# Causal attention tiles of 64 queries in a two-layer attention and FFN kernel: shared score products, a slot ring, and a new order

## The chip, the cores and the metric

The kernel runs on one core of one Trainium2 chip. The metric is device time in microseconds, the median of several executions of the same program. The engines are named as the profile names them: PE (TensorE matmul) and PEld (its weight loads), DVE (VectorE), ACT (ScalarE), POOL (GpSimd) and SP (SyncE, which here issues nearly all DMAs).

## What is computed

Two kinds of layer alternate, attention and a gated FFN, each applied twice to a sequence of 2048 rows of 512 columns (bf16). Attention has 32 heads of 16 columns and works in four segments of 512 rows; each segment has causal softmax attention inside itself and, beside it, a linear memory of the segments before. Cut to what matters:

```python
for s in range(4):                                   # segments of L = 512 rows
    qs, ks, vs = q[:, :, s], k[:, :, s], v[:, :, s]  # 32 heads, Dh = 16
    logits = einsum('bhqd,bhkd->bhqk', qs, ks) * Dh ** -0.5 + causal_mask
    a_dot = einsum('bhqk,bhkd->bhqd', softmax(logits), vs)
    pq = phi(qs)                                     # t + 1 where t > 0, else exp(t)
    a_mem = einsum('bhld,bhde->bhle', pq, M) / (einsum('bhld,bhd->bhl', pq, z)[..., None] + 1e-6)
    outs.append(g * a_mem + (1 - g) * a_dot)         # g = sigmoid(beta), one per head
    pk = phi(ks)
    M = M + einsum('bhld,bhle->bhde', pk, vs); z = z + einsum('bhld->bhd', pk)
...
x = x + A(layernorm(x));  x = x + (gelu(n @ w_gate) * (n @ w_up)) @ w_down   # n = layernorm(x)
x = x + A(layernorm(x));  x = x + (gelu(n @ w_gate) * (n @ w_up)) @ w_down   # n = layernorm(x)
```

## The kernel before

The work is cut into eight steps k: segments 0 to 3 of the first attention and FFN, then of the second. The class `Att` holds the attention of one step and `Ffn` its FFN. All weights, all of x and the memory stay on chip.

**Order.** Nothing is ordered by a scheduler on the chip: `order` walks through the program once, on the host, with a clock for every engine (`Clocks`, `Engine`) and assumed costs. PE's queue is filled one call or product at a time, and the order in which instructions are written is the order in which each engine runs them. Work for PE waits in a list of `Item`s, each with a due time and a condition; a call to `score` goes first where the backlog of exps on ACT is short. Work for the other engines is posted with the time from which it is ready and a slack; if it is posted on two engines, the one that serves it first takes it. The numbers in `POLICY` are due times and slacks. If no item can be opened while scores are still left, the loop writes a product on the tile `warm`, which computes nothing that is used (a fill).

**Attention.** Heads go in quartets. The 128 rows of a q or k block b hold eight heads of 16 rows; four of them, one in each strip of 32 partitions, run side by side in PE as tiles of 32 rows ("rows"). The even heads (par 0) use the upper 16 rows of each strip from `kf`; the odd ones (par 1) use all 32 rows of `kB`, a copy of the keys whose even heads' rows are zero. The copy is made by DVE for steps under 5 (`kb_dve`) and by SP's DMAs, four for each block, after that.

A score product has 128 keys as stationary operand and queries as columns. The causal triangle is cut at 128 queries: for one head, 512 + 384 + 256 + 128 = 1280 columns, five rounds of 256 (`PIECES`), each for a quartet. Eight steps, four blocks, two heads per strip and five rounds make 320 rounds, always two in one `score` call. A call writes four PSUM banks; two exps of 1024 columns (ACT, L1246) move them into slots of `pt_all`, of which there are ten, and POOL zeroes what lies over the diagonal (`affine_select`, L1252). A flush (`flush_item`, L838) multiplies the probabilities of a quartet with its values `vaug`, whose 17th column makes the softmax sum; it runs as four tiles of 32 columns of the array ("columns"), 1280 columns in six groups of four matmuls, and gives its slots back. There are 64 flushes.

**Tilings.** `Clocks.tiling` tracks three tilings of PE: rows, columns and whole. `product` (L396, L399) writes a 128x128 product either whole (L399) or as four column tiles (L396): in columns if PE is in columns already, or if it is in rows and a flush is pending. The memory's products (denominators `den_mm` L671, numerators `num` L694, updates `m` L748) and the transposes `turn_item` (L485 to L487) are always whole.

**Norms.** `Norm` makes statistics and the normalised rows `xn` on DVE; SP's transposing DMAs (`turn_later`) turn them into `xnT`, or PE does for the keys in `BY_PE` (FFN norms of steps 0, 1 and 7).

**phi.** ACT makes the exponential e, POOL cuts it at 1 (L643), DVE adds (L629). The buffers for xn, e and am are separate.

Of the kernel before, what the change touches and what calls it, by code (L numbers as in the profile page):

```python
# [20 lines left out]
H = 32  # L21
# [9 lines left out]
VW = H * (DH + 1)  # L31
SCALE = DH ** -0.5
# [9 lines left out]
NO_DIAG = 1  # L42
# [6 lines left out]
XN_BUFS = 4  # L49
FILL = 2  # L50
# [4 lines left out]
    flush_wait=31.24, piece_slack=21.809, kb_slack=10.712, mem_slack=-1.256, margin=2.578, qk_due=1.366,  # L55
    e_q=-0.208, e_k=1.104, exp_slack=-8.673, e_slack=10.49, phi_slack=11.84, gelu_slack=-0.257, act_evict=7.504,
    first_evict=-5.126, gate_step=0.0, up_due=1.343, up_step=0.018, down_due=3.044, down_step=0.196,
    upd_due=-0.283, v0_due=-0.631, x1_at=2.428, x2_at=1.735, x3_at=6.651, x3_load=17.614, cut_slack=-5.505,
    direct=4, gelu_tiles=1, phi_pool=0, kb_dve=5, rounds=2, early=8.837, starve=0.645, ahead=0.994, near=-6.896,
    cap=1, soon=6.003)  # L60
# [68 lines left out]
class Clocks:  # L129
# [3 lines left out]
    SMALL = 0.025  # L133
    SWITCH = 0.097
# [89 lines left out]
class Item:  # L224


    def __init__(self, due, ready, ops, done, kind, ps, after="start"):
        self.after = after
        self.due, self.ready, self.ops, self.done, self.kind, self.ps = due, ready, ops, done, kind, ps
        self.posted = 0.0  # L230
# [12 lines left out]
class Policy:  # L243
    def __init__(self, values):
        self.__dict__.update(values)


def order(pol, nc, cst, seg, wrk, psp, A_x, A_wq, A_wk, A_wv, A_wo, A_beta, B_x, B_w_gate, B_w_up, B_w_down, out):
# [29 lines left out]
    for cols in (slice(0, P), slice(P, D)):  # L278
        load(w_att["k"][:, :, cols], w_view(A_wk)[:, :, cols])
        load(w_att["q"][:, :, cols], w_view(A_wq)[:, :, cols])  # L280
# [44 lines left out]
    kBs = [cst.tile([P, KT, L], BF16, name=f"kB{i}") for i in range(SETS)]  # L325
    for kB in kBs[1:]:
        nc.vector.memset(kB[:], 0.0)
    maskB = cst.tile([P, 1], F32, name="maskB")
    nc.vector.reduce_sum(out=maskB[:], in_=bd[:, 16:P:32], axis=mybir.AxisListType.X)

    tmp_e = cst.tile([P, H], F32, name="tmp_e")
    tmp_e2 = cst.tile([P, H], F32, name="tmp_e2")
    cden = cst.tile([P, H], BF16, name="cden")
    macc = cst.tile([P, 4, P], F32, name="macc")
    zacc = cst.tile([P, 4], F32, name="zacc")
    vaugs = [cst.tile([P, TPS, VW + 15], BF16, name=f"vaug{i}")[:] for i in range(SETS)]
    vaugs.append(gel_sb[:].rearrange("p f l -> p (f l)")[:, 0:TPS * (VW + 15)].rearrange("p (t v) -> p t v", t=TPS))

    def by_head(va):
        return va[:, :, 0:VW].rearrange("p t (h e) -> p t h e", e=DH + 1)  # L340


    def gate_constants():
        nc.vector.tensor_scalar(out=cden[:], in0=tmp_e[:], scalar1=1.0, scalar2=None, op0=ALU.add)
        nc.vector.tensor_scalar(out=tmp_e2[:], in0=tmp_e2[:], scalar1=1.0, scalar2=None, op0=ALU.add)


    def later_constants():
        def column(va):
            nc.vector.tensor_copy(out=by_head(va)[:, :, :, DH], in_=cden[:].unsqueeze(1).to_broadcast([P, TPS, H]))  # L350
            nc.vector.memset(va[:, :, VW:], 0.0)

        for n, va in enumerate(vaugs[-1:] + vaugs[:-1]):
            ck.dve.post(12.0 + 3.0 * n, NORMAL, (0.4, lambda va=va: column(va), None))

# [34 lines left out]
    def product(out, lhsT, rhs, start=True, stop=True):  # L390

        if ck.mode == "columns" or ck.mode == "rows" and any(it.kind == 'flush' for it in items):
# [4 lines left out]
        else:  # L397
            ck.tiling("whole")
            nc.tensor.matmul(out, lhsT=lhsT, rhs=rhs, start=start, stop=stop)  # L399

# [8 lines left out]

    xn_slots = Slots(ck, XN_BUFS)  # L410

    class Norm:
# [35 lines left out]
        def start(self, ready):  # L448
            self.xnT = seg.tile([P, KT, L], BF16, tag=self.tag, bufs=1, name="xnT")
            for j in range(TPS):  # L450
                xn_slots.take(lambda i, j=j: self.row(j, i, max(ready, ck.pe)))

        def normed(self, j, i):
            xn = seg.tile([P, D], BF16, tag=f"xn{i}", bufs=1, name="xn")
            nc.vector.tensor_scalar(out=xn[:], in0=x_sb[:, self.tt0 + j, :], scalar1=self.mv[:, j, 0:1],  # L455
# [3 lines left out]
        def row(self, j, i, ready):  # L459
            xn = Box(lambda: self.normed(j, i))  # L460

            def landed(t):
                xn_slots.back(i, t)
                self.left -= 1
                if not self.left:
                    ev[self.key] = t

            def told(t):
                if self.key in BY_PE:
# [5 lines left out]
            ck.dve.post(ready, self.slack, (Slowed(0.405, 0.17), xn, told))  # L475

        def turn_item(self, j, xn, t, landed):
# [4 lines left out]
            def turned():  # L482
                return ps()[:, 0:half].bitcast(BF16).rearrange("p (k t) -> p k t", t=P)

            ops = [(Clocks.MM[512] / 2, whole(lambda: nc.tensor.matmul(  # L485
                ps()[:, half:L], lhsT=warm[:], rhs=wide[:, 0:2, :], start=True, stop=True)))] * FILL
            ops += [(Clocks.MM[128], whole(lambda kt=kt: nc.tensor.transpose(  # L487
                turned()[:, kt, :], xn()[:, kt * P:(kt + 1) * P], ident[:]))) for kt in range(KT)]
            return Item(-0.5, lambda: t + Engine.LATENCY <= ck.pe + FILL * Clocks.MM[512] / 2, ops,
# [20 lines left out]
    class Att:  # L510
        def __init__(self, k):
            self.k, self.s, self.tt0 = k, k % NSEG, TPS * (k % NSEG)
            self.norm = Norm(("xnTa", k), self.tt0, f"xnTa{k % 2}", NORMAL, lambda: k < 2 or ("qkv", k - 2) in ev)
            self.vaug = vaugs[(k - 1) % SETS if k else SETS]
            self.ab, self.aT, self.amT, self.n_qkv, self.n_am, self.n_num = {}, None, {}, 0, 0, 0
# [7 lines left out]
        def add_items(self):  # L523
# [5 lines left out]
            def first():  # L529
                if k:  # L530
                    self.q, self.kf = (seg.tile([P, KT, L], BF16, tag=f"{n}{k % SETS}", bufs=1, name=n)
                                       for n in ("q", "kf"))
                    self.kB = kBs[k % SETS]
                else:
                    self.q, self.kf, self.kB = (wd_sb[:, KT * i:KT * (i + 1), :] for i in range(3))
# [839 lines left out]
```

## Time and profile before

| | |
|---|---|
| median of 3 runs | 554.04 us (553.85 to 556.86) |
| the profiled execution | 554.69 us, span 553.0 us, granted PE clock 1.00 |
| exps on ACT (L1246) | 320, 1025 ns each |
| masks on POOL (L1252) | 192 of 128x512, 681 ns; 128 of 128x256, 446 ns |
| score matmuls (L822) | 1536 |
| flush matmuls (L838) | 1536 |
| POOL's cuts of e (L643) | 48, 1545 ns each |

The profiled execution's own time is 1.7 us over its span, which is what the profiler covers. In the lines of the profile, a group names line, engine, operation, tiles written and read, shape and count, and behind the bars busy time, mean duration and idle time before it. Matmuls overlap, so the time that one costs PE is read from the start of one to the start of the next and not from its duration.

### The profile page before, as it was taken

The numbers are of one execution on the slowest core, as the hardware profiler recorded it, in microseconds if no ns is written. First come the engines' busy times: TensorE is split into PE (matmuls) and PEld (weight loads), VectorE is DVE, ScalarE is ACT, GpSimd is POOL, SyncE is SP. The second block draws the span as 40 slices with busy tenths as digits, with TensorE's granted clock in tenths as the row PEclk, the third lists the DMA queues.
The fourth block names the chain that finished last, engine by engine and source line by source line (L and its number), as shares of the span: only waits on it lengthen the run. The fifth ranks groups of instructions, "written<-read, shape, count | busy, mean of one in ns | idle before, by whom it ended". The sixth has DMA issues, their size and how long they took to land.

```text
span 553.0 us, 21391 instructions
## 1 busy us (share of the span) xinstructions
PE 544.8 (99%) x9257; PEld 269.2 (49%) x9257; DVE 449.3 (81%) x837; ACT 445.1 (81%) x570; POOL 280.4 (51%) x410
## 2 busy tenths in 40 slices
PE   8999999999999999999999999999999999999997
PEld 4444454454544545444444445444554446445544
DVE  7999899889978999689896898968978697776062
ACT  5899899999999998999999899999539987930500
POOL 2687767278617877237882356836427264300000
PEclk9999999999999999999999999999999999999999
DMA  8355701510131022301142021021321004100001
GB/s 260 47 118 129 180 3 40 163 13 3 30 59 22 13 50 50 60 3 40 24 56 42 2 47 35 12 41 22 50 67 31 4 4 97 21 2 21 19 2 39
DMA packets 66463, 26.56 MB, mean 48 GB/s; under 512 B 55104, under 2 KB 66368, under 8 KB 66368
## 3 DMA queue, kind: packets, MB, share of 16 engines
q1 hardware_dynamic: 65936, 24.92, 21.3%
q8 instruction: 72, 1.18, 0.9%
q10 hardware_dynamic: 432, 0.27, 0.2%
q14 instruction: 23, 0.19, 0.1%
HBM read 9.71 MB, written 2.10 MB: 21 GB/s over the span
## 4 chain that ended last, share of the span: by engine, by line
PE 79%; DVE 17%; issue 2%; DMA 1%; ACT 0%; POOL 0%; DVEq 0%
PE ps L396 42%; PE ps L399 21%; PE ps L822 7%; PE ps L838 5%; DVE st L425 3%; DVE xn L455 2%; DVE x_sb L908 2%; DVE byq L853 2%; PE ps L694 1%; DVE ab L861 1%; PE ps L748 1%; DMA phik<-e 1%; DVE q L386 1%; DVE mv L433 1%; DVE kf L386 1%
## 5 line engine op out<-in xcount | busy, mean ns | idle before, releaser
L1246 ACT ACTIVATE pt<-ps 128x1024 bf16<-128x1024 f32 x320 | 309.3, 1025 | 44.4 <-PE ps L822 34.5
L1252 POOL TENSOR_SCALAR_AFFINE_SELECT pt<-pt 128x512 bf16<-128x512 bf16 (+1 forms) x320 | 185.7, 587 | 182.8 <-ACT pt L1246 180.2
L968 DVE TENSOR_TENSOR gel_sb<-gel_sb,ps 128x512 bf16<-128x512 bf16 x112 | 76.4, 686 | 47.2 <-PE ps L396 27.5
L643 POOL TENSOR_SCALAR e<-e 128x512 bf16<-128x512 bf16 x48 | 74.1, 1545 | 4.3 <-ACT e L625 1.8
L396 PE MATMUL ps<-xnT,wu_sb 128*32 128x512 bf16 x1280 | 73.5, 380 | 0.0
L396 PE MATMUL ps<-xnT,wg_sb 128*32 128x512 bf16 x1144 | 68.9, 380 | 0.3 <-DVE x_sb L908 0.3
L908 DVE TENSOR_TENSOR x_sb<-x_sb,ps 128x512 bf16<-128x512 bf16 (+1 forms) x68 | 43.0, 643 | 23.9 <-PE ps L399 16.0
L396 PE MATMUL ps<-wd_sb,gel_sb 128*32 128x512 bf16 (+1 forms) x1060 | 60.5, 369 | 0.0
L853 DVE STREAM_TRANSPOSE byq<-ps 128x512 f32<-128x512 f32 x64 | 45.0, 706 | 6.9 <-PE ps L838 6.7
L396 PEld LDWEIGHTS <-wu_sb 128*32 128x32 bf16 x1280 | 32.8, 97 | 33.4 <-issue 2.8
L399 PE MATMUL ps<-wd_sb,gel_sb 128*128 128x512 bf16 (+1 forms) x239 | 45.1, 342 | 0.0
L396 PEld LDWEIGHTS <-wg_sb 128*32 128x32 bf16 x1144 | 28.7, 97 | 28.6 <-issue 5.5
L838 PE MATMUL ps<-pt,vaug 128*32 128x256 bf16 (+1 forms) x1344 | 40.7, 256 | 0.4 <-ACT gel_sb L946 0.3
L425 DVE BATCH_NORM_STATS2 st<-x_sb 128x6 f32<-128x512 bf16 x60 | 40.5, 674 | 0.2
L1020 ACT ACTIVATE gel_sb<-gel_sb 128x512 bf16<-128x512 bf16 x70 | 38.4, 628 | 0.1
L399 PE MATMUL ps<-xnT,wg_sb 128*128 128x512 bf16 x162 | 37.8, 380 | 0.0
L396 PEld LDWEIGHTS <-gel_sb 128*32 128x32 bf16 x1060 | 26.0, 97 | 24.2 <-issue 4.6
L838 PEld LDWEIGHTS <-vaug 128*32 128x32 bf16 x1344 | 31.1, 97 | 10.8 <-issue 2.9
L386 DVE CAST gel_sb<-ps 128x512 bf16<-128x512 f32 x46 | 30.8, 683 | 5.3 <-PE ps L396 4.9
L399 PEld LDWEIGHTS <-gel_sb 128*128 128x128 bf16 x239 | 22.6, 97 | 17.2
L455 DVE TENSOR_SCALAR xn<-x_sb,mv,rs 128x512 bf16<-128x512 bf16 x64 | 30.0, 522 | 1.2 <-POOL rs L443 0.9
L822 PE MATMUL ps<-q,kf 16*128 16x256 bf16 (+1 forms) x672 | 30.7, 255 | 0.0
(129 smaller groups left out, 738.2 us busy)
## 6 DMA issues: line engine op xcount, KB each, us to landing
wg_sb<-in_B_w_gate_dram SPq DMA_DIRECT2D x8, 224.0 KB, 4.4
wu_sb<-in_B_w_up_dram SPq DMA_DIRECT2D x8, 224.0 KB, 4.4
wd_sb<-in_B_w_down_dram SPq DMA_DIRECT2D x7, 256.0 KB, 3.0
x_sb<-in_A_x_dram SPq DMA_DIRECT2D x3, 512.0 KB, 8.1
out_dram<-x_sb SPq DMA_DIRECT2D x12, 128.0 KB, 1.9
xnT<-xn SPq DMA_TRANSPOSE x48, 2.5
kB<-kf SPq DMA_DIRECT2D x48, 16.0 KB, 1.8
wv_sb<-in_A_wv_dram SPq DMA_DIRECT2D x1, 512.0 KB, 7.2
```

What stands on the lines that cost most here:

```text
L386: ck.dve.post(ck.made(), slack, (0.673, lambda: nc.vector.tensor_copy(out=dst(), in_=src()), end), taken=taken)
L396: nc.tensor.matmul(out[r], lhsT=lhsT[:, r], rhs=rhs, start=start, stop=stop, tile_position=(0, 32 * c))
L399: nc.tensor.matmul(out, lhsT=lhsT, rhs=rhs, start=start, stop=stop)
L425: nc.vector.bn_stats(out=self.st6[:, 0, :], in_=x_sb[:, self.tt0 + j, :])
L643: return lambda: eng.tensor_scalar(out=e[0][:], in0=e[0][:], scalar1=1.0, scalar2=None, op0=ALU.min)
L822: nc.tensor.matmul(ps_all[:, pair[unit // 2], o:o + n], lhsT=lhsT[rows, b, P * ki:P * ki + P], rhs=self.q[rows, b, q0:q0 + n], start=True, ...
L838: nc.tensor.matmul(ps()[32 * j:32 * j + 32, q0:q0 + n], lhsT=self.vaug[:, ki, h * (DH + 1):h * (DH + 1) + 32], rhs=pt_all[:, slot, unit, c ...
L853: nc.vector.transpose(out=self.byq[:, par, :, :].rearrange("p a c -> p (a c)"), in_=ps()[:])
L908: ck.dve.post(ck.made(), slack, (0.15 + 0.00104 * (c1 - c0), lambda: nc.vector.tensor_tensor(out=xt, in0=xt, in1=ps()[:, 0:c1 - c0], op=AL ...
L968: ck.dve.post(ck.made(), NORMAL, (0.683, lambda: nc.vector.tensor_tensor(out=g, in0=g, in1=ps()[:], op=ALU.mult), lambda t: (ps.read(t), e ...
L1246: nc.scalar.activation(out=pt_all[:, s0, :, :].rearrange("p (h u) c -> p h (u c)", h=2), in_=ps_all[:, p0[0]:p0[1] + 1, :], func=ACT.Exp, ...
L1252: nc.gpsimd.affine_select(out=half, in_=half, pattern=[[0, w], [1, P]], compare_op=ALU.is_ge, fill=0.0, base=0, channel_multiplier=-1)
```

## The change

- **Tiles of 64 queries.** The part of each head's triangle that lies over full 64-query blocks is laid out in four rounds (`FULL`). What is left is, for each 128 keys, the square over which the diagonal begins: the first 64 keys against the first 64 queries of the same 128. For these, the keys of the even head and of the odd head are put side by side as one stationary operand of 128 columns, so that one product serves both heads (`PAIRED`, the round `SHARED`). A pair of heads has 9 rounds where it had 10: 288 in all.
- **Keys.** In place of `kB` there is `kx`, per block and 128 keys three times 64 columns: the first 64 keys of the even head, then all keys of the odd head. Two copies with a mask as scale make it, on DVE, POOL or ACT (`on_any`).
- **Values.** The shared round's probabilities hold the even head in partitions 0 to 63 and the odd head in 64 to 127. `vz` holds the values for it, half of its rows for the one and half for the other kind of head, zero elsewhere; two SP DMAs per step fill it from `vaug`, after the last flush of the step before. `vaug` is ordered by even and odd heads. A flush has ten groups of four matmuls (six with `vaug`, four with `vz`), again 1280 columns, and waits for `vz`.
- **Slots.** Slot number = round number modulo 10, in a fixed order. One exp takes a pair of banks with both rounds of a call and writes half of each of two neighbouring slots.
- **Masks.** One per round where there is a diagonal (`DIAG`), on POOL; the shared round is masked by DVE (one multiplication with `tri`) or by POOL (two halves).
- **Choice of engine.** xn of attention norms, the cut of e and the addition of the memory's part to aT may be done by DVE or POOL (`on_dve_or_pool`). xn, e and am share six buffers.
- **PE's tilings and turns.** The memory's products go through `product`, and `columns=1` lets products after a score always be in columns. With `pe_turns=1` PE turns segment 1's attention rows, without fills.
- **Order.** A new `POLICY`; values products need only their own 128 rows of xnT, and wo and down products may be opened when their first operand is there (`soon`). The first weights of q and k come in halves of 256 columns.

```diff
-ROUNDS = 5
-STEPS = 8 * ROUNDS
-PIECES = [[(0, 0, 256, 0)], [(0, 256, 256, 0)], [(1, 128, 256, 0)], [(3, 384, 128, 0), (1, 384, 128, 128)],
-          [(2, 256, 256, 0)]]
+ROUNDS = 9
+STEPS = KT * ROUNDS
+C = P // 2
+FULL = [[(0, 64, 256, 0)], [(1, 192, 64, 0), (0, 320, 192, 64)], [(1, 256, 256, 0)], [(3, 448, 64, 0), (2, 320, 192, 64)]]
+DIAG = [1, 1, 0, 2]
+SHARED = len(FULL)
+PAIRED = [(ki, P * ki, C, C * ki) for ki in range(TPS)]
...
-        if ck.mode == "columns" or ck.mode == "rows" and any(it.kind == 'flush' for it in items):
+        if ck.mode == "columns" or ck.mode == "rows" and (pol.columns or any(it.kind == 'flush' for it in items)):
...
+    def on_dve_or_pool(ready, slack, later, fast, slow, emit, told):
+        taken = []
+        ck.dve.post(ready, slack, (fast, lambda: emit(nc.vector), told), taken=taken)
+        if later is not None:
+            ck.pool.post(ready, slack + later, (slow, lambda: emit(nc.gpsimd), told), taken=taken)
...
+    def by_pe(self):
+        return self.key in BY_PE or self.key[0] == "xnTa" and self.key[1] <= pol.pe_turns
...
+                    for which, c0, c1, src, costs in ((0, 0, C, lo[:, :, 0:C], (0.22, 0.9, 0.4)),
+                                                      (1, C, 3 * C, lo, (0.36, 1.6, 0.61))):
+                        on_any(ck.pe, pol.kb_slack if k else NORMAL, pol.kb_pool, pol.kb_act, costs, lambda t2: there(t2),
+                               self.kx[:, b, :, c0:c1], src, masks[:, which:which + 1])
...
+                    for a in range(2):
+                        ck.sp.post(ck.pe, pol.vz_slack, (0.62, lambda a=a: nc.sync.dma_start(
+                            out=half(vz, slice(C * a, C * a + C), a), in_=half(self.vaug, slice(0, C), a)), vz_sent))
+                def vz_sent(t):
+                    self.n_vz += 1
+                    t2 = max(t + 1.8, ck.dma + 1.2)
...
             def den_mm(j, b):
-                nc.tensor.matmul(dens()[:, j, b, :], lhsT=self.phiq[:, b, j * P:(j + 1) * P],
-                                 rhs=mem_state[k - 1][1][:, b, :], start=True, stop=True)
+                product(dens()[:, j, b, :], self.phiq[:, b, j * P:(j + 1) * P], mem_state[k - 1][1][:, b, :])
...
+                work = [(i + par * (SHARED + 1), self.vaug, *piece) for i, pieces in enumerate(FULL) for piece in pieces]
+                work += [(SHARED, vz, *piece) for piece in PAIRED]
+                for m, (i, va, ki, q0, n, c0) in enumerate(work):
+                    for j in range(4):
+                        g = (DH + 1) * (par * H // 2 + 4 * b + j)
+                        nc.tensor.matmul(ps()[32 * j:32 * j + 32, q0:q0 + n], lhsT=va[:, ki * VW + g:ki * VW + g + 32],
+                                         rhs=pt_all[:, places[i], j, c0:c0 + n], start=(m == 0),
+                                         stop=(m == len(work) - 1), tile_position=(0, 32 * j))
...
+    def mask_both(slot):
+        view = pt_all[:, slot, :, :].rearrange("p u (t c) -> p (u t) c", c=C)
+        nc.vector.tensor_tensor(out=view, in0=view, in1=tri[:].unsqueeze(1).to_broadcast([P, 4 * TPS, C]), op=ALU.mult)
...
+    def slot_of(k, t):
+        return (k * STEPS + t) % PT_SLOTS
```

More of the change, by code (lines that the diff above doesn't have):

```diff
@@ L1193, in open_item @@
     def open_item(got, bank):
-        it = min(got, key=lambda it: it.due)
+        it = min(got, key=lambda it: it.due())
         items.remove(it)
@@ L1266, in score, with exp, told @@
-        for a, t, places in flushes:
-            a.flush_item(t // (2 * ROUNDS), t // ROUNDS % 2, places, owner[a.k, t // ROUNDS])
+        s0, left = slots[0], [n]
+        for p, pair in enumerate(pairs):
+            score_banks.update(pair)
+            for i in pair:
+                banks[i] = 1e9
+            def exp(p=p, pair=pair):
+                nc.scalar.activation(
+                    out=pt_all[:, s0:s0 + 2, 2 * p:2 * p + 2, :].rearrange("p r h c -> p h r c"),
+                    in_=ps_all[:, pair[0]:pair[1] + 1, :].rearrange("p h (r c) -> p h r c", r=2), func=ACT.Exp, scale=SCALE)
+            def told(a, pair=pair):
+                score_banks.difference_update(pair)
+                for i in pair:
+                    banks[i] = a
+                left[0] -= 1
+                if not left[0]:
+                    for slot, t, done in marks:
+                        post_mask(slot, t, a, done)
+            ck.act.post(max(begun + 0.4, free), pol.exp_slack, (1.024, exp, told), table="exp")
```

424 lines of the change are left out of this document (229 added, 195 removed).

## The prediction

> **What bounds the kernel now.** I read the page first: busy line, slices and chain.
>
> ```profile
> PE 544.8 (99%) x9257; PEld 269.2 (49%) x9257; DVE 449.3 (81%) x837; ACT 445.1 (81%) x570; POOL 280.4 (51%) x410
> ...
> PE   8999999999999999999999999999999999999997
> ...
> ACT  5899899999999998999999899999539987930500
> ...
> PE 79%; DVE 17%; issue 2%; DMA 1%; ACT 0%; POOL 0%; DVEq 0%
> ```
>
> PE is busy in every slice, ACT drops out after slice 33, and the chain that ended last is PE for 79%. A busy PE is not yet a useful one, so next came the table by stretches:
>
> ```profile
> 0.00:20.00 20.00, 18.61 (x184) 8.47 (x188) 16.16 (x46) 14.40 (x24) 8.02 (x21) 1.00 0.59 185
> 20.00:60.00 40.00, 39.48 (x768) 18.79 (x760) 39.37 (x84) 36.91 (x44) 30.91 (x43) 1.00 0.63 118
> 200.00:250.00 50.00, 50.00 (x933) 24.02 (x929) 41.43 (x77) 45.88 (x61) 26.86 (x39) 1.00 0.24 40
> 350.00:400.00 50.00, 49.66 (x925) 24.26 (x924) 42.85 (x76) 42.42 (x57) 27.02 (x38) 1.00 0.22 33
> 500.00:525.00 25.00, 25.00 (x222) 13.61 (x214) 7.37 (x18) 8.89 (x15) 1.27 (x2) 1.00 0.07 22
> ```
>
> Columns: length, busy PE, PEld, DVE, ACT, POOL, granted clock (1.00 throughout). PE has no free time in any stretch after 20 us, also where ACT and DVE have plenty (500 to 525). So the time is the sum of what PE is given, and the change must be priced in PE time. What one piece costs is read off the starts in the timeline and the chain:
>
> ```profile
> 200.12 0.72 PE L838 MATMUL ps<-pt,vaug 128*32 128x256 bf16 x24
> 200.78 0.40 PE L822 MATMUL ps<-q,kB 32*128 32x128 bf16 x12
> 201.11 2.77 PE L396 MATMUL ps<-wd_sb,gel_sb 128*32 128x512 bf16 x48
> 203.81 0.40 PE L822 MATMUL ps<-q,kf 16*128 16x256 bf16 x8
> ...
> 204.69 0.56 PE L671 MATMUL ps<-zcols,phiq 128*128 128x8 bf16 x16
> 205.10 1.02 PE L399 MATMUL ps<-wd_sb,gel_sb 128*128 128x512 bf16 x4
> ```
> ```profile
> 141.61 0.22 PE ps L487 x4
> ...
> 428.81 10.57 PE ps L396 x196
> ```
>
> The last two lines are pieces of the chain. The 428.81 piece's 196 matmuls are 49 groups of four that run side by side: 10.57 / 49 = 0.2157 us for 512 columns, 0.42 ns a column. A call of two score rounds starts at 200.78 and the next work at 201.11: 0.33 us, of which 512 columns are 0.213; 0.117 is the change out of the row tiling. The 12 groups behind it take 12 x 0.2157 = 2.59 of the 2.70 us to 203.81: 0.11 is the change into it. **One score call costs PE 0.33 + 0.11 = 0.44 us, half of it tiling changes.** Going through the trace's matmuls in order I find 160 such calls.
>
> **The change, part by part, in PE time.** The profiled run took 554.69 us (span 553.0, 1.7 around it), 0.65 above the median 554.04; sums are against 554.69.
>
> *Scores.* Five rounds per head of a quartet, ten per pair of heads, become nine: 320 rounds to 288, 160 calls to 144. 16 x 0.44 = **-7.0 us**. The streamed columns are in that (2560 to 2304 per pair, 32 pairs, 3.4 us); the rest is 32 tiling changes.
>
> *Smaller pieces.* A pair's score rounds go from 12 groups of four to 16, a flush from 6 to 10; flush columns stay 1280. That is 32 x 4 + 64 x 4 = 384 more groups. A group costs about 2.5 ns beyond its columns (0.2157 against 0.2133 at 2.4 columns a ns): **+1.0**. 640 groups then have 64 columns (8 x 32 in scores, 6 x 64 in flushes), which no row of before shows. From below: L671's 16 matmuls of 8 columns start 0.41 us before the next work, 25.6 ns each with a weight load each. From above: L487's 128 columns take 0.22 / 4 = 55 ns. By length 64 columns are 26.7 + 2.5 = 29 ns; I take that, as the 8-column row shows that loads alone don't need more. At 55 ns it would be 640 x 26 ns = 16.6 us more. Cover for it: the loads must keep hiding behind the group before.
>
> The Trainium skill (TensorE: Matmul & The Clock Gate, Back-to-back issue gap) speaks against such cutting: for a stream of load and matmul pairs it gives about 81 ns a matmul at 128 columns and 131 at 512, so that small ones cost far more than their columns. If 64 columns cost that 81 too, the 640 groups would take some 33 us over my 29 ns (an estimate from that page). L487's 55 ns, each with its own load, disagree with it here.
>
> *Tiling kept.* den, num and update (L671, L694, L748) now go through `product`, which stays in column tiling, and `columns=1` picks it after every score. In the trace's order 30 changes lie between whole and column tiling; at 0.11 (204.14 to 204.69 is two groups, 0.432, and 0.118) I let 18 go: **-2.0**. Against it: 96 L671 matmuls become 96 groups of four; at 25.6 to 55 ns each that is 0 to 2.8 us; I take **+0.5**. Bounds of the part -3.3 to +1.
>
> *Fills.* PE is also given work that does nothing:
>
> ```profile
> L396 PE MATMUL ps<-warm 128*32 128x512 bf16 x72 | 4.7, 381 | 0.0
> ...
> L399 PE MATMUL ps<-warm 128*128 128x512 bf16 x7 | 1.8, 381 | 0.0
> ```
> ```profile
> L396 PE MATMUL ps<-warm x72: 378/379/391, 21.0 to 28.8; 128*32 128x512 bf16 x72
> L399 PE MATMUL ps<-warm x7: 378/379/390, 26.6 to 142.5; 128*128 128x512 bf16 x7
> ```
>
> 18 + 7 fills x 0.2157 = 5.4 us, nearly all between 21.0 and 28.8. There segment 1's rows wait for SP's four transposing DMAs, issued from 19.98; its first q product runs at 28.98. With `pe_turns=1` PE turns them itself: 16 transposes x 0.055 = 0.9 and some three tiling changes, 0.3. Fills gone -4.5; net **-3.3** (bounds 0 and -5.4). What is late next there is the eviction of the turned rows, four times 0.41 to 0.61 us over DVE and ACT, which is why I leave one us of fills.
>
> *vz.* The first flush of each segment now waits for two SP copies of 64 partitions (139 KB by shape), posted when the segment's values and the last flush of the segment before are there. Behind that flush in PE's queue stands everything. The kernel's order counts on 0.62 + 1.8 us. Nearest rows: kB<-kf, 16 KB, 1.8 us; out, 128 KB, 1.9; wd, 256 KB, 3.0. So 0 to 0.6 us late, seven or eight times: 0 to 5; I take **+1.0**, as 128 KB is the nearest size. SP gets easier: 48 kB copies go, 16 come, and four turns of segment 1 leave it.
>
> *Costed at nothing, and the cover.* ACT loses 32 exps of 1025 ns, 32.8 us. POOL's masks: 4 of 256 elements (446 ns) and 2 of 512 (681) per pair of heads, 32 x 3.15 = 101 us where it had 185.7; shared rounds are 1024 elements in two halves, by the step from 446 to 681 about 1.15 each, 37 us if it takes half of them. DVE: the other shared masks (L871's 512 ns for 512 elements, so 0.5 to 1.0 for 1024; 16 x 0.8 = 13), its share of key copies and of the cuts of e (L568: 426 ns for 512), some 12: 449 to about 474 of 544, 87%. Cover: evictions free banks PE writes next; if DVE is late PE stands, rival A. The 10-slot ring gives back slots in order, but for nine rounds a pair, so it holds as much work as before. Stalls that are in the trace now (4.8 us after the start, the longest 1.5 us at 59.3 to 60.8 on phik<-e) I leave as they are: their DMA path is unchanged. Start and last 3.5 us: the same.
>
> Sum: -7.0 + 1.0 - 2.0 + 0.5 - 3.3 + 1.0 = **-9.8**: 544.9 profiled, 544.2 on the median's scale; I say 544.
>
> **The rivals.**
> *A. New waits take most of it.* vz at its late bound (+4 over my term) and DVE past 87% making PE wait for banks, 3 us more: 544 + 7 = 551. For: DVE is 39.37 of 40 busy from 20 to 60, where the first copies and masks fall. Against: POOL and ACT both lose work and are offered the same copies. 0.15, about half of it below 551.3.
> *B. Slower: 64-column groups show their loads.* In scores and flushes, 640 times. At L487's 55 ns: 544 + 16.6 = 561; a load's own 97 ns (L838's weight loads) would give 640 x 68 ns more, 588. It decides from 29 + 10 / 0.64 = 45 ns a group, where the gain is gone. Against: 25.6 ns at L671, though those loads are of the whole array and one per matmul, where here are four of a tile each. 0.10. The skill's 81 ns, named above, would land here.
> *C. More than I sum.* All fills, half the stalls and 28 of the 30 tiling changes go, and vz is on time: 544 - 2.1 - 2.4 - 1.1 - 1.0 = 537.5. For: ACT, which ran 90 to 95% in most stretches up to 350, has 33 us less to do, so PE finds work oftener. 0.10.
> *D. It doesn't do what it says.* The new order spends the 10 us on fills and bare PE elsewhere: 554. For: the order is written anew from other costs throughout. Against: from 29 to 549 us PE had something to do nearly always; less work in all must then end earlier. 0.05.
>
> **How the numbers follow.** Forecast 0.60. About 0.5%, 2.8 us, is what a measurement of this kernel can tell from no change: faster is below 551.3, slower above 556.8. Faster: 0.60 + 0.10 + 0.09 of A = 0.79. Same: 0.06 of A and 0.05 of D, 0.11. Slower: B, 0.10. The range runs from C's end with its spread, 536, to just past A, 552.5; B, D and C's lower tail are left out, 0.18.
>
> **What would show it.** L822's matmuls in 144 calls, about 0.44 us each from the work before to the work after; exps x288; a flush of 40 matmuls from its start to the next work in some 0.67 us (0.66 now), and 64-column groups 29 ns apart; warm fills in column tiling nearly gone between 21 and 29 us; the first flush of each segment without idle time released by a DMA into vz; DVE below 90%. The forecast is wrong if PE shows bare time in the stretches from 60 to 500, or if 64-column groups stand 45 ns or more apart.

## The result, and the profile after

The changed kernel takes 557.76 us (median of 16 runs, 556.41 to 560.54) against 555.25 (16 runs of before, 553.85 to 558.0): ratio 1.0045, interval 1.0028 to 1.0062. It is 2.5 us slower, where 10 us less were forecast. The profiled execution of after took 560.54 us (span 558.9), 2.8 over its median; experiments 3 and 4 below have the same order and the same time, and their profiled executions, at 557.7, are nearer to the typical one.

The page of after, cut to the lines that answer to those of before:

```profile
PE 540.9 (97%) x12801; PEld 292.7 (52%) x12806; DVE 457.4 (82%) x845; ACT 427.8 (77%) x518; POOL 290.8 (52%) x357
...
PE   8999999999899989999999999999999999999997
...
PEclk9999999999899989999999999999999999999999
...
PE 68%; DVE 19%; issue 5%; POOL 3%; ACT 2%; DMA 2%; SPq 0%; DVEq 0%; ACTq 0%; POOLq 0%
```

The share of PE in the chain fell from 79 to 68%, that of "issue" rose from 2 to 5% and that of DVE from 17 to 19%. PE now has two slices under 9 in mid-span, the 11th (140 to 154 us) and the 15th (196 to 210), and in the same two the granted clock (PEclk) drops, where before showed 9 throughout. The table by stretches (length, then busy PE, PEld, DVE, ACT, POOL, then the granted clock) shows where:

```profile
20.00:60.00 40.00, 36.97 (x952) 19.22 (x947) 38.15 (x78) 37.16 (x47) 34.24 (x42) 1.00 0.51 112
100.00:150.00 50.00, 47.04 (x1221) 26.18 (x1217) 46.90 (x87) 42.33 (x50) 35.59 (x41) 0.97 0.27 64
200.00:250.00 50.00, 48.60 (x1254) 25.49 (x1253) 40.44 (x73) 45.92 (x55) 22.79 (x30) 0.97 0.26 43
350.00:400.00 50.00, 48.88 (x1256) 26.00 (x1249) 43.19 (x77) 42.95 (x48) 28.33 (x35) 1.00 0.14 26
```

Not busy, PE is 3.0, 3.0, 1.4 and 1.1 us there, where before had 0.5, 0.4, 0.0 and 0.3. From 20 to 60 DVE has 38.15 of 40, less than the 39.37 of before, and still PE loses most there. So DVE's busy share does not show what happened; single instructions do.

What was to be seen of the cheap part is there. The timeline of after at a flush (start, length, engine, line):

```profile
300.87 0.40 PE L923 MATMUL ps<-q,kx 32*128 32x256 bf16 x12
...
301.20 0.83 PE L452 MATMUL ps<-xnT,wg_sb 128*32 128x512 bf16 x12
...
301.86 0.62 PE L939 MATMUL ps<-pt,vaug 128*32 128x256 bf16 x24
...
302.30 0.29 PE L939 MATMUL ps<-pt,vz 128*32 128x64 bf16 x16
...
302.42 0.61 PE L452 MATMUL ps<-xnT,wg_sb 128*32 128x512 bf16 x8
```

The flush's 40 matmuls run from 301.86 to 302.42, 0.56 us (here without a change of tiling behind them; with 0.11 for one it is the forecast's 0.67), and the four groups of 64 columns start at 302.300, .328, .357 and .387: 29 ns apart.

Going through both traces' matmuls in order, and giving each group its columns' time (0.42 ns a column and 2.5 ns, which gives the 215.7 ns read at 512 columns and the 29 ns at 64), a change of tiling at most 0.105 us, and what is then left to "bare" (over 0.15 us at once) or to "small gaps", PE's time divides so:

| us of PE's time | before | after | experiment 4 (same time as after) |
|---|---|---|---|
| score columns | 35.1 | 32.0 | 32.0 |
| tiling changes | 35.3 (350) | 29.9 (293) | 29.9 (293) |
| flushes | 35.1 | 35.7 | 35.7 |
| fills | 5.4 (25 groups) | 1.9 (9) | 1.9 (9) |
| bare | 7.7 | 22.4 | 19.7 |
| small gaps | 6.2 | 8.4 | 7.3 |

Scores, tiling changes and flushes fell by 7.9 us together, fills by 3.5. PE's own turns added 0.9. That is the forecast's 10 us, and it is there. Bare time gave 12 to 15 us of it back. (The trace of after lacks 5 of its 12806 matmuls, so about 1 us of its bare time may be work without a record; that of experiment 4 has them all.)

Where such a piece of bare time comes from is seen at 196 us. The timeline of after:

```profile
195.86 0.83 POOL L1311 TENSOR_SCALAR_AFFINE_SELECT pt<-pt 128x512 bf16<-128x512 bf16 x1
196.08 3.62 DVE L523 TENSOR_SCALAR xn<-x_sb,mv,rs 128x512 bf16<-128x512 bf16 x4
...
196.65 2.38 POOL L1316 TENSOR_SCALAR_AFFINE_SELECT pt<-pt 64x1024 bf16<-64x1024 bf16 x2
...
198.36 0.28 PE L923 MATMUL ps<-q,kx 32*128 32x256 bf16 x2
...
199.63 0.67 DVE L1011 TENSOR_TENSOR x_sb<-x_sb,ps 128x512 bf16<-128x512 bf16 x1
...
200.35 0.40 PE L923 MATMUL ps<-q,kx 32*128 32x256 bf16 x10 [1.71 <-DVE x_sb L1011]
```

Four xn rows take DVE 3.62 us, 0.9 each, while POOL masks the two halves of a shared round beside them. Then only can DVE add the down product to x_sb and free its bank, and PE, after two matmuls of a score call, stands 1.71 us for that bank. The chain of after through the same stretch says the same, and what came behind:

```profile
196.08 3.62 DVE xn L523 x4
199.71 0.60 DVE x_sb L1011
200.31 0.04 issue
200.35 0.40 PE ps L923 x7
200.75 0.67 PE ps L939 x40
201.42 2.49 PE ps L452 x24
```

The last line is six groups of 512 columns in 2.49 us, 0.415 each: half of the usual speed (0.2157). From 201.4 on, after PE had stood, the granted clock is 0.50 for 3.4 us, and so it is from 143.3. These drops are not the loss: the six executions of after that kept a clock of 1.00 took 557.15 us in the median (556.41 to 557.43), still above the 555.25 of all executions of before; the three with the lowest clock, 0.994, took 560.05.

### The profile page after: what moved, and what is told of

It is laid out like the page before. It is cut to its first block, busy times and chain, and to the rows that moved or that the text cites. A ratio compares the mean times of both kernels' runs of the same rounds, so it can differ in the third digit from the quotient of the medians.

```text
span 558.9 us, 28332 instructions
## 1 busy us (share of the span) xinstructions
PE 540.9 (97%) x12801; PEld 292.7 (52%) x12806; DVE 457.4 (82%) x845; ACT 427.8 (77%) x518; POOL 290.8 (52%) x357
## 4 chain that ended last, share of the span: by engine, by line
PE 68%; DVE 19%; issue 5%; POOL 3%; ACT 2%; DMA 2%; SPq 0%; DVEq 0%; ACTq 0%; POOLq 0%
PE ps L452 49%; PE ps L455 8%; PE ps L923 5%; PE ps L939 4%; DVE xn L523 3%; DVE byq L956 2%; DVE st L493 2%; DVE x_sb L1011 2%; ACT pt L1364 2%; DVE gel_sb L1073 1%; DVE ab L964 1%; DVE aT L971 1%; DMA amT<-am 1%; DVE gel_sb L442 1%; DVE e L730 1%
## 5 line engine op out<-in xcount | busy, mean ns | idle before, releaser
L1364 ACT ACTIVATE pt<-ps 128x1024 bf16<-128x1024 f32 x288 | 277.9, 1026 | 38.0 <-PE ps L923 32.2
L1311 POOL TENSOR_SCALAR_AFFINE_SELECT pt<-pt 128x256 bf16<-128x256 bf16 (+1 forms) x192 | 108.6, 581 | 135.4 <-ACT pt L1364 129.0
L452 PE MATMUL ps<-xnT,wg_sb 128*32 128x512 bf16 x1568 | 95.9, 380 | 0.8 <-DVE gel_sb L442 0.6
L452 PE MATMUL ps<-wd_sb,gel_sb 128*32 128x512 bf16 (+1 forms) x1568 | 88.3, 365 | 0.0
L1316 POOL TENSOR_SCALAR_AFFINE_SELECT pt<-pt 64x1024 bf16<-64x1024 bf16 x44 | 53.1, 1206 | 13.9 <-ACT pt L1364 12.4
L1125 ACT ACTIVATE gel_sb<-gel_sb 128x1536 bf16<-128x1536 bf16 (+1 forms) x28 | 37.0, 1378 | 0.1
L923 PE MATMUL ps<-q,kx 32*128 32x64 bf16 (+2 forms) x1120 | 32.5, 217 | 3.8 <-DVE x_sb L1011 1.7
L939 PE MATMUL ps<-pt,vaug 128*32 128x256 bf16 (+2 forms) x1344 | 34.8, 238 | 1.3 <-DVE x_sb L1011 1.3
L452 PE MATMUL ps<-xnT,wq_sb 128*32 128x512 bf16 x496 | 33.8, 385 | 1.3 <-ACT pt L1364 0.7
L452 PE MATMUL ps<-xnT,wk_sb 128*32 128x512 bf16 x496 | 35.0, 387 | 0.0
```

The lines of the kernel that those rows point to most:

```text
L452: nc.tensor.matmul(out[r], lhsT=lhsT[:, r], rhs=rhs, start=start, stop=stop, tile_position=(0, 32 * c))
L923: nc.tensor.matmul(ps_all[:, bank, o + c0:o + c0 + n], lhsT=lhsT, rhs=self.q[rows, b, q0:q0 + n], start=True, stop=True, tile_position=(32 ...
L939: nc.tensor.matmul(ps()[32 * j:32 * j + 32, q0:q0 + n], lhsT=va[:, ki * VW + g:ki * VW + g + 32], rhs=pt_all[:, places[i], j, c0:c0 + n], ...
L1311: nc.gpsimd.affine_select(out=view, in_=view, pattern=[[0, 4], [0, n], [1, C]], compare_op=ALU.is_ge, fill=0.0, base=C, channel_multiplier=-1)
L1316: nc.gpsimd.affine_select(out=view, in_=view, pattern=[[0, 4 * TPS], [1, C]], compare_op=ALU.is_ge, fill=0.0, base=0, channel_multiplier=-1)
L1364: nc.scalar.activation(out=pt_all[:, s0:s0 + 2, 2 * p:2 * p + 2, :].rearrange("p r h c -> p h r c"), in_=ps_all[:, pair[0]:pair[1] + 1, :] ...
```

## The theory and its rivals

**H (hold).** While POOL runs a long mask, a DVE instruction that reads and writes rows on chip does not get on; it ends when POOL's instruction does. xn sorted by what POOL does beside it (whole trace, DVE's mean durations in ns; cases with several kinds beside them are left out, but for one):

| POOL beside xn | before | after |
|---|---|---|
| nothing | 402 (15 instructions) | 404 (10) |
| masks of rounds (0.45 to 0.68 us) | 571 (35) | 580 (20), up to 749 |
| a half mask (64x1024, 1.2 us) | none | 1224 (2); with a round mask too 972 (4), up to 1284 |
| a cut of e (tensor_scalar, 1.55 us) | 540 (5), up to 803 | 593 (5), up to 767 |
| POOL's own xn (2.1 us) | none | 530 (11), up to 852 |
| the first norm's pow of two elements (0.75 us) | 408 (2) | 408 (2) |

Beside masks, 24 of the 26 xn in after and 26 of 35 in before end 0.14 to 0.15 us after a mask does. The others, at about 400 ns, had begun 0.1 us or more ahead of the mask; the 128x512 masks that began 0.10 to 0.16 us after such an xn took 0.75 to 0.80 us, where 0.68 is the mean. So the hold goes both ways, and whoever is first wins.

The order of both kernels knows of this in part, and the prediction passed over it. `Slowed(0.405, 0.17)` puts an xn down for 0.405 us, and for 0.17 more beside POOL's cuts, copies, additions and xn. A mask on POOL adds nothing there. Summed over all its instructions, DVE took some 20 us longer than the order's costs in after and some 17 in before; the longest overrun of an xn is 0.88 us in after and 0.46 in before.

**P (POOL late).** POOL's half masks come late for the flush. **V**: the first flush of a segment waits for vz. **S**: the late start (first scores at 11.59 instead of 10.30 us) is passed on to the end. **O**: the order is bad whatever the instructions cost.

## The experiments

In experiments 1 to 7 the order is that of after, so only the edited instructions differ.

**1. All of POOL's masks and its other long operations short.** Masks on one of four units or 8 of 64 columns, cuts and additions on 64 of 512.

```diff
-  view = pt_all[:, slot, :, 0:C * n].rearrange("p u (t c) -> p u t c", c=C)
+  view = pt_all[:, slot, :, 0:C * n].rearrange("p u (t c) -> p u t c", c=C)[:, 0:1]
...
-  view = pt_all[C * h:C * h + C, slot, :, :].rearrange("p u (t c) -> p (u t) c", c=C)
+  view = pt_all[C * h:C * h + C, slot, :, :].rearrange("p u (t c) -> p (u t) c", c=C)[:, :, 0:8]
...
+  ...(e[0][:, 0:64] if eng is nc.gpsimd else e[0][:]), summed)
...
+  c = slice(0, 64 if eng is nc.gpsimd else L)
+  eng.tensor_tensor(out=self.aT[:, b, c], in0=self.aT[:, b, c], in1=self.amT[b][:, c], op=ALU.add)
```

> The changed kernel with every instruction in the same order on every engine; POOL's masks, cuts of e and additions to aT work on a fraction of their columns (masks of the full rounds on one of four units, the two halves of the shared round on 8 of 64 columns, cuts and additions on 64 of 512), so these parts of the computation are left out. Theory T (POOL's longer instructions hold up DVE's instructions that work in SBUF alone; DVE falls behind the order that was fixed beforehand, frees banks late, and PE stands bare): DVE's xn fall from 585 ns to under 450, PE's bare time after the start from 18 us to under 8, the time from 557.8 to 545 to 550. Rival C (the order leaves PE no reserve, whatever DVE and POOL do): 554 to 558, bare time 14 us or more.

Measured: 543.80 us, ratio 0.9788 (0.9763 to 0.9812). POOL's busy time falls from 290.8 to 152.5 us, and DVE's, with the same 845 instructions, from 457.4 to 435.3:

```profile
PE 532.8 (98%) x12806; PEld 288.8 (53%) x12806; DVE 435.3 (80%) x845; ACT 426.6 (79%) x518; POOL 152.5 (28%) x357
```

Bare time after the first 12 us falls from 18.2 (15.5 in experiment 4) to 3.1 us. 14 us hang on POOL's instructions; H and P are both still possible.

**2. The half masks alone short.**

```diff
-  view = pt_all[C * h:C * h + C, slot, :, :].rearrange("p u (t c) -> p (u t) c", c=C)
+  view = pt_all[C * h:C * h + C, slot, :, :].rearrange("p u (t c) -> p (u t) c", c=C)[:, :, 0:8]
```

> The changed kernel in the same order; only POOL's two halves of the shared round's mask (44 instructions of 1.2 us) work on 8 of 64 columns, the rest of that mask is left out. Theory T: these are the longest instructions that DVE has to wait behind, so xn over 1 us disappear and the time falls by 3 to 6 us, to 552 to 555. Rival C: within 1 us of 557.8.

Measured: 549.80 us, 0.9896 (0.9871 to 0.9921): 8.0 us, more than I expected, from 44 instructions that fell from 1206 to 448 ns each. PE's bare time after the first 12 us falls to 8.4. The rest of experiment 1's 14 us lies with the round masks, cuts and additions. xn's lines (shortest, median, longest of 59; first after, then this kernel):

```profile
L523 DVE TENSOR_SCALAR xn<-x_sb,mv,rs x59: 374/537/1284, 7.5 to 511.1; 128x512 bf16<-128x512 bf16 x59
```
```profile
L523 DVE TENSOR_SCALAR xn<-x_sb,mv,rs x59: 373/411/855, 7.5 to 500.7; 128x512 bf16<-128x512 bf16 x59
```

**3. vz's copies of one partition.**

```diff
-  out=half(vz, slice(C * a, C * a + C), a), in_=half(self.vaug, slice(0, C), a)), vz_sent))
+  out=half(vz, slice(C * a, C * a + C), a)[0:1], in_=half(self.vaug, slice(0, C), a)[0:1]), vz_sent))
```

> The changed kernel in the same order; the two copies into vz move one partition in place of 64, the rest of vz stays zero, so the shared rounds' even and odd values are left out. Rival V (PE waits for vz at the first flush of each segment): 3 to 5 us less, 553 to 555. Theory T: about 1 us less (the trace shows one flush that waits for it, 0.7 us, and one late landing may hide behind another wait).

Measured: 557.72 us, 1.0043 (1.0028 to 1.0059), as after. V falls: vz costs nothing that can be measured.

**4. The first weights in a piece of 128 columns and one of 384**, to bring the first scores forward.

```diff
-    for cols in (slice(0, D // 2), slice(D // 2, D)):
+    for cols in (slice(0, P), slice(P, D)):
```

> The changed kernel in the same order; the first weights of k and q come as 128 and 384 columns, as before the change, in place of 256 and 256. Rival S (part of the loss is at the start: the first scores begin 1.0 us later than before because the first weights take 5.6 us to land where they took 4.2): 1.0 us less, 556.8. If the start is bound by something else: no change.

Measured: 557.68 us, 1.005 (1.0031 to 1.0068); the first scores still start at 11.60. It tells nothing of S, as it did not move what it was to move.

**5. vz zeroed ahead of DVE's other preparations.** In after DVE zeroes vz for 1.88 us right before the first statistics.

```diff
+    vz = cst.tile([P, VALUES], BF16, name="vz")
+    nc.vector.memset(vz[:], 0.0)
...
-    vz = cst.tile([P, VALUES], BF16, name="vz")
-    nc.vector.memset(vz[:], 0.0)
```

> The changed kernel; the only edit is that DVE zeroes vz (1.88 us) before it sums the two masks and not after, since the sums wait for POOL until 2.40 us. In the trace DVE's first statistics start at 4.83 in the changed kernel and at 3.70 in the one before, and PE's first transposes 1.0 us later. Rival S' (this is the late start, which narrower first weights didn't move): statistics at about 3.7 and the time 1.0 us less, 556.7. Otherwise no change.

Measured: 557.70 us, 1.0035 (1.0017 to 1.0053). The statistics start at 3.53 us instead of 4.83 and the first transposes at 6.70 instead of 7.94, but the wait at 22.5 us grows from 1.13 to 1.33 us and nothing is left at the end. The first scores start at 11.02, so about half of the 1.3 us was won back there, and none of it arrives. S falls as far as this half goes.

**6. The half masks as pow operations on four elements.** POOL is kept about as long, but hardly touches data.

```diff
-  nc.gpsimd.affine_select(out=view, in_=view, pattern=[[0, 4 * TPS], [1, C]], compare_op=ALU.is_ge,
-                          fill=0.0, base=0, channel_multiplier=-1)
+  view = pt_all[C * h:C * h + C, slot, 0, 0:TPS]
+  nc.gpsimd.tensor_tensor(out=view, in0=view, in1=mhalf[C * h:C * h + C, :, 0], op=ALU.pow)
```

> The changed kernel in the same order; each half mask of the shared round on POOL is replaced by a power of 4 elements a partition, which in the trace takes POOL about 1.05 us against 1.2 but moves almost no data; the halves' masking is left out. This parts two readings of the run with short halves (549.8 us). Theory T (DVE is held up beside a half mask; in the trace xn take 404 ns alone, 1224 beside a half and 408 beside a power): about as short as the run with short halves, 549 to 552. Rival P (POOL itself is late, so masks come late and flushes wait): most of the loss stays, 555 to 557.

Measured: 549.71 us, 0.9893 (0.9872 to 0.9914): the same 8 us as experiment 2. This run decides between H and P. From its page (columns: count, busy us, mean ns, idle before), then its xn:

```profile
PE 538.0 (98%) x12806; PEld 291.4 (53%) x12806; DVE 448.3 (82%) x845; ACT 427.6 (78%) x518; POOL 283.2 (52%) x357
...
L1316 POOL TENSOR_TENSOR pt<-pt,mhalf 64x4 bf16<-64x4 bf16 x44 | 46.1, 1049 | 6.4 <-ACT pt L1363 4.7
```
```profile
L523 DVE TENSOR_SCALAR xn<-x_sb,mv,rs x59: 366/404/853, 7.5 to 499.4; 128x512 bf16<-128x512 bf16 x59
```

POOL is busy as long as in after, within 8 us, and each of the 44 operations takes 1049 ns where the half mask took 1206. Yet nine xn that run beside such a pow take 400 ns on average, as with POOL idle, and DVE's busy time falls by 9.1 us. A POOL instruction that takes nearly as long (0.16 us less) but moves no rows does no harm. What cost 8 us is the hold on DVE, not POOL's lateness; experiment 7 bears this out, where POOL needs 0.19 us more for each half mask and the kernel is faster. P falls for the half masks; for the other six of experiment 1's 14 us, hold and lateness were not told apart.

**7. Each half mask in two pieces** of 64x512, 696 ns each, in place of 1206 for both.

```diff
-  nc.gpsimd.affine_select(out=view, in_=view, pattern=[[0, 4 * TPS], [1, C]], compare_op=ALU.is_ge, ...)
+  for u in range(0, 4, 2):
+      view = pt_all[C * h:C * h + C, slot, u:u + 2, :].rearrange("p u (t c) -> p (u t) c", c=C)
+      nc.gpsimd.affine_select(out=view, in_=view, pattern=[[0, 2 * TPS], [1, C]], compare_op=ALU.is_ge, ...)
```

> The changed kernel in the same order and with the whole computation; each half mask on POOL is written as two instructions of 64x512, so POOL has more to do (about 2 x 0.67 for 1.2 us) but none of its masks is long. Theory T: DVE waits for shorter pieces; a gain of 1 to 4 us, 554 to 557. Rival P: POOL gets later, no gain or up to 2 us slower, 557.5 to 560.

Measured: 556.33 us, 1.0012 (0.9995 to 1.0029). The longest xn falls to 901 ns, but seven that meet a piece still take 718 on average, and more pieces meet more instructions. Bare time after 12 us is 14.3. Of 8 us 1.4 come back: the sum of the hold counts, not only its longest case.

**8. Before, with POOL's masks and cuts short** (one unit, 64 of 512 columns), in before's own order.

```diff
-  half = pt_all[:, slot, first:4:2 if w == 2 else 1, 0:P]
-  nc.gpsimd.affine_select(out=half, in_=half, pattern=[[0, w], [1, P]], compare_op=ALU.is_ge, ...)
+  half = pt_all[:, slot, first:first + 1, 0:P]
+  nc.gpsimd.affine_select(out=half, in_=half, pattern=[[0, 1], [1, P]], compare_op=ALU.is_ge, ...)
...
+  v = slice(0, 64 if eng is nc.gpsimd else L)
```

> The kernel before the change, same order; POOL's masks work on one of their units and the cuts of e on 64 of 512 columns, so these parts of the computation are left out. It asks how much of what the same cut gave in the changed kernel (14 us) was there before. Theory T (it is the longer POOL instructions and the order without reserve of the changed kernel): 2 to 5 us less than the kernel before, 550 to 553. Rival B (the kernel before lost as much beside POOL, and the change's loss is elsewhere): 10 us or more less, 545 or below.

Measured: 553.18 us (550.13 to 554.25), 0.9952 (0.9929 to 0.9975). Before loses some 2 to 3 us beside POOL where after loses 14. Yet DVE was held almost as much in before:

```profile
PE 542.6 (99%) x9257; PEld 267.9 (49%) x9257; DVE 432.3 (79%) x837; ACT 444.7 (81%) x570; POOL 148.9 (27%) x410
```

Its busy time falls by 17.0 us (from 449.3), in experiment 1 by 22.1. So the amount of the hold alone does not make the difference. What is left is where it falls, that is whether PE is waiting behind DVE at that moment; this is argued, not shown. With POOL out of the way the two algorithms compare as 553.18 to 543.80, -9.4 us, near the forecast's -9.8; the seven runs here lie between 550.13 and 554.25, so the nearness is no better than some 2 us.

The last four runs compute the whole, and ask what the hold costs if the order knows of it. They change the order throughout, so a gain of theirs is not tied to one instruction.

**9. An order that counts the hold**, with after's POLICY. A mask on POOL holds DVE's marked instructions until 0.14 us after its end. Other costs are set to what the trace of after shows too (POOL's xn, additions and half masks, key copies, DVE's shared mask, vz's landing), a memory product on DVE is marked as well, and vz is zeroed first. So this run does not part the hold from the other costs.

```diff
+class Locking(float):
+    pass
...
-                if self.rival.port > t + 0.1:
+                if self.rival.lock > t + 0.1:
+                    t = max(t, self.rival.lock + 0.14 - cost)
+                elif self.rival.port > t + 0.1:
                     t += cost.more
                 self.port = t + cost
+            if isinstance(cost, Locking):
+                if self.rival.port > t + 0.1:
+                    t += 0.1
+                self.lock = t + cost
...
-  ck.pool.post(at, NORMAL, (1.12, lambda: mask_half(slot, 0), None), (1.12, ...
+  ck.pool.post(at, NORMAL, (Locking(1.15), lambda: mask_half(slot, 0), None), (Locking(1.15), ...
-  ck.pool.post(at, NORMAL, (0.22 + 0.226 * n, lambda: mask(slot, n), done.append))
+  ck.pool.post(at, NORMAL, (Locking(0.22 + 0.226 * n), lambda: mask(slot, n), done.append))
```

> The changed kernel with the whole computation and the recorded policy, ordered anew by clocks that count what the traces show: DVE's instructions in SBUF alone end no earlier than 0.14 us after a POOL mask that runs beside them; POOL's xn 2.1, additions to aT 1.19, key copies 0.93 on POOL and 0.51 and 0.73 on ACT, vz 0.6 us later; vz is zeroed first. Theory T: the order no longer promises what DVE can't keep, so PE's bare time after the start falls from 18 us to under 10 and the time to 549 to 554. Rival C (DVE and POOL simply have too much to do): 555 to 560.

Measured: 551.64 us, 0.993 (0.991 to 0.9951). Bare time after 12 us is 5.9, but fills rise from 9 to 39 groups of 0.2157 us, 8.4 us, most of them here (four matmuls a group, and 11 whole ones beside):

```profile
L462 PE MATMUL ps<-warm x112: 379/379/390, 72.0 to 463.7; 128*32 128x512 bf16 x112
```

The order now sees the holes and fills them with nothing useful; 6.1 us of the 14 come back.

**10. The same with POLICY searched anew** under these clocks.

```diff
-    flush_wait=21.427, piece_slack=9.862, kb_slack=32.535, mem_slack=-5.228, margin=1.888, qk_due=0.887,
+    flush_wait=2.93, piece_slack=1663.28, kb_slack=1411.667, mem_slack=4.321, margin=2.2, qk_due=0.33,
...
```

> As the run that is ordered by counted waits, with the policy's due times and slacks searched again under these clocks. Theory T: bare time after the start under 8 us, 546 to 551, faster than both kernels. Rival C: 554 or more.

Measured: 548.51 us (547.33 to 551.71), 0.9883 (0.9854 to 0.9913): faster than both kernels.

```profile
PE 535.5 (98%) x12879; PEld 290.1 (53%) x12879; DVE 456.2 (83%) x837; ACT 426.1 (78%) x510; POOL 309.3 (57%) x359
```

DVE is as busy as in after, POOL busier (309.3 us against 290.8), and the hold is as large (xn's longest 1287 ns). PE still has 17 fills (3.7 us) and 7.9 us bare after the first 12. The hold was not taken away; other work was put where it falls.

**11. Control: after's own clocks, POLICY searched**, vz zeroed first.

```diff
-    flush_wait=21.427, piece_slack=9.862, kb_slack=32.535, mem_slack=-5.228, margin=1.888, qk_due=0.887,
+    flush_wait=6.206, piece_slack=1.963, kb_slack=2954.778, mem_slack=-0.084, margin=1.888, qk_due=1.429,
...
```

> The control for the tuned order: the changed kernel with vz zeroed first and its own, uncounted clocks, the policy searched again for as long as one of the two searches behind the counted order. It parts the counting from the searching. Theory T: an order that is searched under clocks that know nothing of POOL's holds loses again what it promises: 553 to 559, bare time after the start over 14 us. Rival Q (any new search gives the gain): 546 to 551, like the counted and searched order.

Measured: 554.30 us, 0.9989 (0.9971 to 1.0006), with 14.6 us bare after 12 us. O is part of it: another order under the same wrong costs is 3.5 us better than after. It leaves the bare time about where it was (15.5 in experiment 4), and 5.8 us of experiment 10's 9.2 over after came only with the counted costs. How much of these is the hold and how much the other costs set in experiment 9 was not run; and the control had one search where experiment 10 had two.

**12. Experiment 10 with each half mask in two pieces.**

```diff
+        for u in range(0, 4, 2):
+            view = pt_all[C * h:C * h + C, slot, u:u + 2, :].rearrange("p u (t c) -> p (u t) c", c=C)
```

> The counted and searched order (548.5 us), same order of instructions, with each half mask written as two instructions of 64x512. In the changed kernel that gave 1.4 us. Theory T: 0 to 2 us less, 546.5 to 548.5, as that order leaves fewer DVE instructions beside a half mask; if POOL's own time decides there, 549 to 551.

Measured: 548.88 us, 0.9898 (0.9876 to 0.992): no gain over experiment 10. Where the order already allows for the hold, cutting it finer brings nothing.

## Why the prediction was wrong

**The sum of PE's work was right.** Score columns, tiling changes, flushes: -7.0 + 1.0 - 2.0 = -8.0 forecast, -7.9 in the table. The denominators' 96 groups, forecast at +0.5, took some 33 ns each in experiment 4 in place of 25.6: +0.8. Fills and turns: -3.3 forecast, -3.5 + 0.9 = -2.6. 57 tiling changes went, where I had 32 + 18. With POOL's operations short the kernel takes 543.80 us; 544 was forecast. That this agrees to 0.2 us is luck: the run leaves out work that the forecast counted, before gains 2 to 3 us by the same cut, and terms that were off (fills, vz) offset each other.

**64-column groups (rival B)** stand 29 ns apart, the value taken. The Trainium skill's spacing of about 81 ns for a matmul of 128 columns with its load (TensorE: Matmul & The Clock Gate, Back-to-back issue gap) is not borne out for tiles in this kernel: row tiles of 128 columns, each with its load, start 55 to 57 or 65 to 68 ns apart in nearly all calls of before.

**vz** was costed at +1.0. It lands in 2.9 us (136 KB; I went by 1.9 for 128 KB), and one flush waits visibly, 0.7 us at 237.7; experiment 3 makes it 0.

**The start** was costed at nothing. It moved by 1.3 us; the half of it that experiment 5 won back was worth nothing.

**The step that failed is "Costed at nothing, and the cover".** I asked whether DVE has time for what it gets, found 474 us (87%) and called that enough. It got less than that, 457.4 (82%), and PE still stood, because the delay is in single instructions at moments when a bank is awaited. For the same reason rival A had the right place (PE waiting for banks behind DVE, 20 to 60 us first) at the wrong price and on the wrong condition: I gave it 3 us from DVE's load and 4 from vz, and 0.15; some 14 us hang on POOL's instructions, 8 of them shown to be the hold, and DVE stood at 82%. No rival of mine had the hold. The sign that I had named, bare PE time between 60 and 500 us, is what the table by stretches shows.

The trace of before would have shown it. Its xn, all of one shape, were not of one length:

```profile
L455 DVE TENSOR_SCALAR xn<-x_sb,mv,rs x64: 316/450/864, 6.4 to 504.9; 128x512 bf16<-128x512 bf16 x64
```

402 ns alone and 571 beside the masks, with the end tied to the mask's end, say that each mask holds DVE until it is done, unless xn began first. The change puts masks of 1.2 us (44 of them, 53.1 us in all; I let POOL have half the shared rounds, 37 us) in place of ones of 0.68. I priced them on POOL, where there was room, and not on DVE. From the row one could have bounded the xn beside a half mask at 1.2 us, which is what it took. The Trainium skill has the rule (SBUF — State Buffer, Who interferes with whom): GpSimd and some VectorE instructions share a pair of ports, and whichever starts first keeps the other out for the whole instruction. xn's 1224 ns beside a half mask agrees with it, as do the masks that were late behind an xn; the 593 ns beside POOL's cuts of 1.55 us do not. I did not weigh that rule.

**Rival D was judged by the wrong argument.** "Less work in all must then end earlier" holds if the order's costs hold. By the order's own clock the last matmul starts at 543.4 us in before and 535.0 in after: the change was worth 8.4 us on paper. In the traces they start at 549.2 and 555.7, some 6 and 21 us late (18 in experiment 4, 3 in experiment 1). The counted orders keep their word better: 542.2 promised and 546.6 in the trace in experiment 9, 536.3 and 543.3 in experiment 10; the control promised 533.1 and came at 548.2. An order that is written out beforehand cannot react: each late instruction delays everything queued behind it.

Open: how much of the round masks', cuts' and additions' six us is hold; and why PE in after feels as 14 us what cost before 2 to 3, with DVE held nearly as much. The longer half masks are 8 of it; that the new order leaves PE less in reserve is a guess.

## What to carry to other kernels

Before work is moved onto an engine with free time, sort the durations of one shape on its neighbour by what runs beside them: a spread such as 316/450/864 for one shape is a price that no busy share shows. Price a longer instruction also at what it holds up elsewhere, and look for whoever waits behind that. Where an order is fixed beforehand by assumed costs, compare its own clock with the trace; the difference shows what there is to gain without less work. Here 9 us of it came back by counting the hold and other measured costs and searching again.

## What the runs showed of the hardware

- A POOL affine_select holds DVE's xn until 0.14 to 0.15 us after its own end: 404 ns alone, 580 beside masks of 0.45 to 0.68 us, 1224 beside one of 1.2 us. An xn that began 0.1 us or more ahead of the mask is not held (about 400 ns), and a 128x512 mask that follows it by 0.10 to 0.16 us is longer (0.75 to 0.80 us for 0.68). A POOL tensor_scalar of 1.55 us holds xn much less (593 on average, 767 at most in after), as does POOL's own xn of 2.1 us (530, 852 at most); a pow of four elements, 1.05 us, not at all (400, experiment 6).
- In a group of four column tiles, 64 columns cost 29 ns with a load for each tile.
- After PE had stood for 1.7 us at 198.6, six groups ran at half speed, 2.49 us, at a granted clock of 0.50. In experiment 4 PE stood 1.9 us at the same place (from 196.5) and the six groups behind it took 1.29 us, full speed, so the drop does not follow from the wait's length alone.
